# Agent attention with a squared-ReLU layer: sessions of three, three and two slots instead of two

## The chip, the cores and the metric

The kernel runs on one core of a Trainium2 chip (trn2). The metric is the device time of one execution in microseconds. Five engines work side by side, each with its own queue in order: PE (TensorE, matrix products), ACT (ScalarE), DVE (VectorE), POOL (GpSimd) and SP, which only starts DMAs. PEld stands for PE's loading of weights, which the profile lists apart. PE writes into PSUM, which has eight banks of 128 rows x 512 fp32 values; POOL works on SBUF alone.

## The reference

There are four batches of 12480 tokens of width 128, with 49 agents each, and then one layer of width 2048 over all 49920 tokens:

```python
a2k = sm(agents, k)          # softmax of agents . k / sqrt(128) over the keys
agent_v = a2k @ v
q2a = sm(q, agents)
x = (q2a @ agent_v).reshape(49920, 128)
h = np.maximum(x @ w_in, 0.0)
out = h * h @ w_out
```

Everything is fp32, and `w_in`, `w_out` come as 64-bit floats.

## The kernel before, in words

For each batch `x @ w_in` is not computed from `x`. The kernel makes a table `agent_v @ w_in` of 49 rows and 2048 columns, and the 49 attention weights of a token multiply it. To keep fp32's precision with matrix products of lower precision (`F32R`), tables, weights and squares are each split into a high part (rounded) and a low part (the rest), and products of parts are added up in PSUM. High and low rows of the attention weights and of the table are stacked: 98 rows, and of the third combination (high weights by low table) 30 rows more, which fill the 128 rows of the array. The other 19 rows of that combination have no room; they are multiplied in a small product of its own. Four copies of these 19 rows lie at rows 0, 32, 64 and 96 (tile `x`, tables `aw_ex`), so that four small products, each on 32 rows of the array, stand side by side.

The tokens are worked in groups of 960, two halves of 480 each. A **slot** is one half and two of the 16 chunks of 128 columns of `w_in`, so a half has 8 slots (`NP`) and the program 832. For each slot `k`:

- `first` multiplies: into a tile `h` of PSUM (two banks, 2 x 480 columns) go two full products of `w` and `aw_hi` and two small ones of `x` and `aw_ex`. Before, `first(k)` does so for two slots at once: four full products, then the four small ones.
- `hidden` makes `r = relu(h)` on ACT, the square on DVE as `r * h` (into SBUF tile `gg` for the even slot, back into PSUM for the odd one), its rounded high part `g_hi` as ACT's own square of `r`, and the low part `g_lo`, square less `g_hi`: two instructions of 480 columns on POOL for the even slot, one of 960 on DVE for the odd one.
- `second` multiplies the parts of the square by `wo_hi` and `wo_lo` into one bank `o`: six full products a slot, added up over the 8 slots of a half. `copied_out` then brings `o` to SBUF on DVE and out.

So a session of two slots has 16 full products of 480 columns and one set of four small ones. `second` of a slot runs `LAG` = 4 slots, two sessions, behind its `first`.

PSUM: three tiles `h` of two banks (`ps_h`), one bank for `o` (`ps_o`) and one (`ps_a`) for all other products. These others are the background: for the next batch the scores of keys, their maxima, the values and tables (`background`, paced by `goal` and `SPREAD`), and for the next group of tokens its queries (`queries`). They are cut into steps at each `yield`, and the loop at the end takes some of them in each slot. The products of `first`, the rectifications, squares, parts and `second` are chained in the order of the program on each engine (`queued`); the background's instructions, and POOL's, are placed between them by the scheduler when the program is built, and then stand fast. `first`'s small products are issued with high priority, right behind its full ones.

The prologue up to about 114 us loads and splits the weights and does the first batch's attention (`alone`).

Of the kernel before, what the change touches and what calls it, by code (L numbers as in the profile page):

```python
# [9 lines left out]
F32 = mybir.dt.float32  # L10
F32R = mybir.dt.float32r
# [6 lines left out]
P = 128  # L18
# [4 lines left out]
G = BLK // 2  # L23
RB = 2
HB = 5
LB = 4
GB = 2
LAG = 4
# [8 lines left out]
def agent_attention_relu2(ctx: ExitStack, tc: tile.TileContext, qT, kT, v, agT, w_in, w_out, outT):  # L37
# [17 lines left out]
    def queued(issue, eng, *args, **kw):  # L55

        with tc.issue_after(chain[eng]) if eng in chain else ExitStack():
            ins = issue(*args, **kw)  # L58
        chain[eng] = ins.ins
        return ins  # L60
# [315 lines left out]
    def first(k):  # L376

        g, i = divmod(k, SLOTS)
# [3 lines left out]
        hs = [ps_h.tile([P, 2, 512], F32, name="h") for _ in range(2)]  # L382
# [5 lines left out]
        with tc.high_priority():  # L388
            for t, out in enumerate(outs):
                rows = slice(t * 32, t * 32 + NL)  # L390
                queued(nc.tensor.matmul, nc.tensor, out, state[b]["lo"][rows, c // 2, :], x[rows, :], start=False, stop=True)
        return hs

    def hidden(k, h):
        r = ffn.tile([P, 2, G], F32, name="r", bufs=RB)
        queued(nc.scalar.activation, nc.scalar, r, h[:, :, :G], AF.Relu)

        gg = h[:, :, :G] if k % 2 else ffn.tile([P, 2, G], F32, name="gg", bufs=GB)
        queued(nc.vector.tensor_mul, nc.vector, gg, r, h[:, :, :G])
        hi = ffn.tile([P, 2, G], F32R, name="g_hi", bufs=HB)  # L400
        queued(nc.scalar.activation, nc.scalar, hi, r, AF.Square)
        lo = ffn.tile([P, 2, G], F32R, name="g_lo", bufs=LB)
        if k % 2:
            queued(nc.vector.tensor_sub, nc.vector, lo, gg, hi.bitcast(F32))
        else:
            for n in range(2):
                nc.gpsimd.tensor_sub(lo[:, n, :], gg[:, n, :], hi[:, n, :].bitcast(F32))  # L407
        parts[k] = hi, lo
# [108 lines left out]
    for k in range(total + LAG):  # L517
        if k < total:
# [13 lines left out]
        if k % 2 == 0:  # L532
            hs = first(k) if k < total else ()
            if hs:
                hidden(k, hs[0])
            for n in range(2):
                if k + n >= LAG:
                    second(k + n - LAG)
            copied_out()
            if hs:  # L540
                hidden(k + 1, hs[1])
# [35 lines left out]
```

## Time and profile before

| what | value |
|---|---|
| median of 3 runs | 2089.64 us (2088.23 to 2092.76) |
| the profiled execution, its own time | 2089.47 us |
| its span in the trace | 2087.6 us |
| `r`, ACT, 128x960 | 832 times, mean 962 ns |
| `g_hi`, ACT (square of `r`), 128x960 | 832 times, mean 1007 ns |
| square into PSUM (`h<-r,h`) and into SBUF (`gg<-r,h`), DVE | 416 times each, mean 1160 and 1149 ns |
| `g_lo<-h,g_hi`, DVE, 128x960 | 416 times, mean 1156 ns |
| `g_lo<-gg,g_hi`, POOL, 128x480 | 832 times, mean 1222 ns |
| full products `h<-w` and `o<-g` | 1664 and 4992 |
| small products `h<-x` | 1664 |

A group's row in the profile names the line, the engine, the operation, the tile written and those read, the shapes and the count, then the busy time and the mean of one, then the engine's idle time ahead of these instructions and what ended it. Most rows have line 58, the helper `queued`, so the tiles tell them apart. In a timeline a row has its start, its length, and the count of instructions that it merges. Recorded matmuls overlap: the next starts before the end of the last is recorded.

### The profile page before, as it was taken

Reading aid. Unit: us, or ns where it says so; the run is one execution under the profiler, and the core shown is the slowest. Engines: PE = TensorE matmul, PEld = TensorE weight load, DVE = VectorE, ACT = ScalarE, POOL = GpSimd, SP = SyncE. Lnnn points to the kernel's source line nnn. Section 1 sums busy time; section 2 is a strip of 40 time slices with the busy share of each in tenths; the row PEclk is TensorE's granted clock in tenths of the full one; section 3 lists DMA queues with packets and bytes.
Section 4 is the critical chain, followed back from the end, with each engine's and each line's share of the span. In section 5 each row is a group of like instructions: output and inputs, shape, how many; then the busy total and the mean of one; then the engine's idle time right before and its main releaser. Section 6 shows DMA issues by size and latency. Waiting matters only on the chain. (4 is left out here: it accounts for less than half of the span.)

```text
span 2087.6 us, 31676 instructions
## 1 busy us (share of the span) xinstructions
PE 2051.5 (98%) x10932; PEld 1621.5 (78%) x10932; DVE 1672.7 (80%) x1835; ACT 1775.2 (85%) x2100; POOL 1275.1 (61%) x1110
## 2 busy tenths in 40 slices
PE   8889999999999999999999999999999999999999
PEld 8857777777778877777778877777777777777777
DVE  3465888889887788888887788888888888888887
ACT  1265899989888899999898889999889999989897
POOL 1643587766554477776555458777556565656565
PEclk6588999999999999999999999999999999999999
DMA  8132222121112212221112211221111111111100
GB/s 300 46 118 87 70 75 75 52 65 63 53 56 79 65 53 80 63 60 61 63 40 71 88 35 60 68 75 41 44 51 35 46 35 47 35 47 35 38 23 20
DMA packets 55943, 131.34 MB, mean 63 GB/s; under 512 B 6712, under 2 KB 35336, under 8 KB 55784
## 3 DMA queue, kind: packets, MB, share of 16 engines
q1 hardware_dynamic: 55784, 129.33, 19.3%
q8 instruction: 87, 1.43, 0.3%
q14 instruction: 72, 0.59, 0.1%
HBM read 80.97 MB, written 25.56 MB: 51 GB/s over the span
## 5 line engine op out<-in xcount | busy, mean ns | idle before, releaser
L407 POOL TENSOR_TENSOR g_lo<-gg,g_hi 128x480 fp32r<-128x480 f32 x832 | 999.1, 1222 | 711.2 <-DVE gg L58 457.5
L58 ACT ACTIVATE r<-h 128x960 f32<-128x960 f32 x832 | 800.7, 962 | 145.5 <-PE h L58 132.7
L58 ACT ACTIVATE g_hi<-r 128x960 fp32r<-128x960 f32 x832 | 837.5, 1007 | 34.8 <-PE o L58 1.0
L58 DVE TENSOR_TENSOR h<-r,h 128x960 f32<-128x960 f32 x416 | 482.5, 1160 | 156.7 <-ACT r L58 151.6
L58 DVE TENSOR_TENSOR gg<-r,h 128x960 f32<-128x960 f32 x416 | 478.0, 1149 | 85.4 <-ACT r L58 79.9
L58 PE MATMUL o<-g_hi,wo_hi 128*128 128x480 f32 x1664 | 539.2, 405 | 0.0
L58 DVE TENSOR_TENSOR g_lo<-h,g_hi 128x960 fp32r<-128x960 f32 x416 | 481.0, 1156 | 48.3 <-ACT g_hi L58 7.7
L58 PE MATMUL h<-w,aw_hi 128*128 128x480 f32 x1664 | 485.4, 398 | 10.7 <-DVE gg L58 7.7
L58 PE MATMUL o<-g_hi,wo_lo 128*128 128x480 f32 x1664 | 495.4, 379 | 0.0
L58 PE MATMUL o<-g_lo,wo_hi 128*128 128x480 f32 x1664 | 494.7, 378 | 0.0
L58 PEld LDWEIGHTS o<-g_hi,wo_hi 128*128 128x128 f32 x1664 | 280.9, 188 | 117.4 <-issue 69.5
L58 PEld LDWEIGHTS o<-g_hi,wo_lo 128*128 128x128 f32 x1664 | 313.3, 188 | 47.2
L58 PEld LDWEIGHTS o<-g_lo,wo_hi 128*128 128x128 f32 x1664 | 313.3, 188 | 46.7
L58 PEld LDWEIGHTS h<-w,aw_hi 128*128 128x128 f32 x1664 | 289.3, 190 | 59.3 <-DVE gg L58 20.3
L58 PE MATMUL h<-x,aw_ex 19*128 19x480 f32 x1664 | 207.9, 481 | 1.3 <-DMA x<-w 1.0
L58 PEld LDWEIGHTS h<-x,aw_ex 19*128 19x128 f32 x1664 | 81.6, 182 | 142.4 <-issue 138.1
L334 PEld LDWEIGHTS psa<-ag,qt 128*120 128x120 f32 x816 | 100.6, 184 | 6.5 <-issue 0.7
L58 DVE COPY ob<-o 128x480 f32<-128x480 f32 x104 | 68.2, 656 | 35.9 <-PE o L58 35.5
L334 PE MATMUL psa<-ag,qt 128*120 128x49 f32 x816 | 95.9, 261 | 0.0
L219 POOL TENSOR_TENSOR vs<-vt,vs 128x1024 fp32r<-128x1024 f32 (+1 forms) x39 | 81.6, 2094 | 12.6 <-ACT vs L217 12.3
L183 PEld LDWEIGHTS psa<-ag,kt 128*128 128x128 f32 (+1 forms) x588 | 76.4, 195 | 3.6
L183 PE MATMUL psa<-ag,kt 128*128 128x49 f32 (+1 forms) x588 | 72.7, 271 | 0.0
(112 smaller groups left out, 1069.0 us busy)
## 6 DMA issues: line engine op xcount, KB each, us to landing
qt<-in_qT SPq DMA_DIRECT2D x52, 480.0 KB
out_T<-ob SPq DMA_DIRECT2D x104, 240.0 KB
kt<-in_kT SPq DMA_DIRECT2D x36, 512.0 KB
vt<-in_v SPq DMA_DIRECT2D x36, 512.0 KB
x<-w SPq DMA_DIRECT2D x416, 35.6 KB
ahead<-in_kT SPq DMA_DIRECT2D x12, 512.0 KB
ahead<-in_v SPq DMA_DIRECT2D x12, 512.0 KB
w<-w SPq DMA_DIRECT2D x104, 56.2 KB
```

The costliest lines, as they stand in the source:

```text
L58: ins = issue(*args, **kw)
L183: pe.matmul(sv[:, t, :], kt[:, t * rows : (t + 1) * rows], ag[:, b, :], start=True, stop=True)
L219: eng.tensor_sub(out[:, :, n : n + w], x, out[:, :, :w].bitcast(F32))
L334: pe.matmul(sv[:, t, :], qt[:, t * TP : (t + 1) * TP], ag[:, b, :], start=True, stop=True)
L407: nc.gpsimd.tensor_sub(lo[:, n, :], gg[:, n, :], hi[:, n, :].bitcast(F32))
```

## The change

Eight slots of a half are now worked in sessions of three, three and two (`RUN` = 3). `first`, `second` and the three parts of `hidden` (now `rectified`, `squared`, `split_up`) take a whole session, and `second` follows two sessions behind (`LAG` = 2). A session of three has six full products into all three tiles `h`, then its six small products. The square stays in the SBUF tile where the rectification was put (`g`, in place), for all slots; `g_hi` is a copy of it, not ACT's own square; and of a session the second slot's `g_lo` is DVE's, from two SBUF tiles, while POOL makes the first's and the third's, five of eight in all. The tile `gg` is gone, and buffers of `g_hi` and `g_lo` are 6 each.

```diff
-RB = 2
-HB = 5
-LB = 4
-GB = 2
-LAG = 4
+RUN = 3
+RB = 4
+HB = 6
+LB = 6
+LAG = 2
...
-    def first(k):
+    def first(ks):
-        g, i = divmod(k, SLOTS)
+        g, i = divmod(ks[0], SLOTS)
...
-        hs = [ps_h.tile([P, 2, 512], F32, name="h") for _ in range(2)]
+        hs = [ps_h.tile([P, 2, 512], F32, name="h") for _ in ks]
...
-            for t, out in enumerate(outs):
+            for n, out in enumerate(outs):
+                u, t = divmod(2 * c + n, NQ)
                 rows = slice(t * 32, t * 32 + NL)
-                queued(nc.tensor.matmul, nc.tensor, out, state[b]["lo"][rows, c // 2, :], x[rows, :], start=False, stop=True)
+                queued(nc.tensor.matmul, nc.tensor, out, state[b]["lo"][rows, u, :], x[rows, :], start=False, stop=True)
-    def hidden(k, h):
-        r = ffn.tile([P, 2, G], F32, name="r", bufs=RB)
-        queued(nc.scalar.activation, nc.scalar, r, h[:, :, :G], AF.Relu)
-
-        gg = h[:, :, :G] if k % 2 else ffn.tile([P, 2, G], F32, name="gg", bufs=GB)
-        queued(nc.vector.tensor_mul, nc.vector, gg, r, h[:, :, :G])
-        hi = ffn.tile([P, 2, G], F32R, name="g_hi", bufs=HB)
-        queued(nc.scalar.activation, nc.scalar, hi, r, AF.Square)
-        lo = ffn.tile([P, 2, G], F32R, name="g_lo", bufs=LB)
-        if k % 2:
-            queued(nc.vector.tensor_sub, nc.vector, lo, gg, hi.bitcast(F32))
-        else:
-            for n in range(2):
-                nc.gpsimd.tensor_sub(lo[:, n, :], gg[:, n, :], hi[:, n, :].bitcast(F32))
-        parts[k] = hi, lo
+    def rectified(hs):
+        gs = []
+        for h in hs:
+            g = ffn.tile([P, 2, G], F32, name="g", bufs=RB)
+            queued(nc.scalar.activation, nc.scalar, g, h[:, :, :G], AF.Relu)
+            gs.append(g)
+        return gs
+
+    def squared(ks, hs, gs):
+        for h, g in zip(hs, gs):
+            queued(nc.vector.tensor_mul, nc.vector, g, g, h[:, :, :G])
+
+    def split_up(ks, gs):
+        for n, (k, g) in enumerate(zip(ks, gs)):
+            hi = ffn.tile([P, 2, G], F32R, name="g_hi", bufs=HB)
+            queued(nc.scalar.copy, nc.scalar, hi, g)
+            lo = ffn.tile([P, 2, G], F32R, name="g_lo", bufs=LB)
+            if n == 1:
+                queued(nc.vector.tensor_sub, nc.vector, lo, g, hi.bitcast(F32))
+            else:
+                for m in range(2):
+                    nc.gpsimd.tensor_sub(lo[:, m, :], g[:, m, :], hi[:, m, :].bitcast(F32))
+            parts[k] = hi, lo
...
-    for k in range(total + LAG):
-        if k < total:
+    sessions = [
+        range(k + n, min(k + n + RUN, k + NP)) for k in range(0, total, NP) for n in range(0, NP, RUN)
+    ]
+    for s in range(len(sessions) + LAG):
+        ks = sessions[s] if s < len(sessions) else ()
+        for k in ks:
...
-        if k % 2 == 0:
-            hs = first(k) if k < total else ()
-            if hs:
-                hidden(k, hs[0])
-            for n in range(2):
-                if k + n >= LAG:
-                    second(k + n - LAG)
-            copied_out()
-            if hs:
-                hidden(k + 1, hs[1])
+        if ks:
+            hs = first(ks)
+            gs = rectified(hs)
+            squared(ks, hs, gs)
+        if s >= LAG:
+            for k in sessions[s - LAG]:
+                second(k)
+        copied_out()
+        if ks:
+            split_up(ks, gs)
```

PE's queue late in the last batch, before: one session of two slots, with `h` numbered by its buffer; `x2` counts the two products of a slot.

```order
L58 MATMUL h_20864<-w1_20582,aw_hi_15370 128x480 x2
L58 MATMUL h_20865<-w1_20582,aw_hi_15370 128x480 x2
L58 MATMUL h_20864<-x1_20583,aw_ex_15371 128x480 x2
L58 MATMUL h_20865<-x1_20583,aw_ex_15371 128x480 x2
L58 MATMUL o_20806<-g_hi_20801,wo_hi_108 128x480 x2
L58 MATMUL o_20806<-g_hi_20801,wo_lo_109 128x480 x2
L58 MATMUL o_20806<-g_lo_20803,wo_hi_108 128x480 x2
L58 MATMUL o_20806<-g_hi_20822,wo_hi_108 128x480 x2
L58 MATMUL o_20806<-g_hi_20822,wo_lo_109 128x480 x2
L58 MATMUL o_20806<-g_lo_20824,wo_hi_108 128x480 x2
```

The same queue of the changed kernel near its end, a session of three and the first two slots of the `o` products behind it:

```order
L58 MATMUL h_20549<-w1_20235,aw_hi_15086 128x480 x2
L58 MATMUL h_20550<-w1_20235,aw_hi_15086 128x480 x2
L58 MATMUL h_20551<-w1_20235,aw_hi_15086 128x480 x2
L58 MATMUL h_20549<-x1_20236,aw_ex_15087 128x480 x2
L58 MATMUL h_20550<-x1_20236,aw_ex_15087 128x480 x2
L58 MATMUL h_20551<-x1_20236,aw_ex_15087 128x480 x2
L58 MATMUL o_20521<-g_hi_20491,wo_hi_108 128x480 x2
L58 MATMUL o_20521<-g_hi_20491,wo_lo_109 128x480 x2
L58 MATMUL o_20521<-g_lo_20493,wo_hi_108 128x480 x2
L58 MATMUL o_20521<-g_hi_20496,wo_hi_108 128x480 x2
L58 MATMUL o_20521<-g_hi_20496,wo_lo_109 128x480 x2
L58 MATMUL o_20521<-g_lo_20498,wo_hi_108 128x480 x2
```

Six small products now stand in a row where four stood, between six full ones and the `o` products of a session two back. In all 832 slots there are 312 sets (208 of six, 104 of four) where there were 416 of four.

DVE's queue around one query of the last batch, before (`m`, `e`, `z` are the query's maximum, difference and sum):

```order
L58 TENSOR_TENSOR g_lo_19982<-h_19947,g_hi_19980 128x960
L337 TENSOR_REDUCE m_20436<-psa_20386 120x8
L339 TENSOR_TENSOR e_20438<-psa_20386,m_20436 120x392
L58 TENSOR_TENSOR gg_19998<-r_19996,h_19986 128x960
L58 TENSOR_TENSOR h_19987<-r_20017,h_19987 128x2x480
L344 TENSOR_REDUCE z_20480<-e_20438 120x8
L58 TENSOR_TENSOR g_lo_20022<-h_19987,g_hi_20020 128x960
```

DVE's queue of the changed kernel around a query of the last batch:

```order
L58 TENSOR_TENSOR g_lo_19682<-g_19652,g_hi_19680 128x960
L337 TENSOR_REDUCE m_20107<-psa_20042 120x8
L339 TENSOR_TENSOR e_20109<-psa_20042,m_20107 120x392
L58 TENSOR_TENSOR g_19710<-g_19710,h_19695 128x960
L344 TENSOR_REDUCE z_20112<-e_20109 120x8
L58 TENSOR_TENSOR g_19712<-g_19712,h_19696 128x960
L345 TENSOR_SCALAR z_20112<-z_20112 120x8
L58 TENSOR_TENSOR g_19714<-g_19714,h_19697 128x960
L346 RECIPROCAL z_20112<-z_20112 120x8
L58 TENSOR_TENSOR g_lo_19744<-g_19712,g_hi_19742 128x960
```

Three squares of a session stand together with one `g_lo` behind them, which reads two SBUF tiles (`g`, `g_hi`) where it read PSUM and SBUF (`h`, `g_hi`); the query's sums `z` stand between the squares.

## The prediction

> **What bounds the kernel now.** The page comes first: who is busy, and at what clock.
>
> ```profile
> PE 2051.5 (98%) x10932; PEld 1621.5 (78%) x10932; DVE 1672.7 (80%) x1835; ACT 1775.2 (85%) x2100; POOL 1275.1 (61%) x1110
> ...
> PEclk6588999999999999999999999999999999999999
> ```
>
> TensorE is busy 98% of the span and holds the full clock after the first tenth. Busy matmuls overlap, though, so the waits are read next, cut to 130 to 2087 us, behind the start.
>
> ```profile
> PE h L58 <- DVE gg L58: 7.4, 12, 1.6
> ```
>
> That is the longest wait of PE itself: 7.4 us in all for a free PSUM tile. So time is won only by giving TensorE less to do, and lost by a new wait of TensorE. What it does is read in the timeline of the last, undisturbed stretch, where two whole sessions of two slots follow each other (I read starts, since the recorded ends overlap).
>
> ```profile
> 2065.75 1.03 PE L58 MATMUL h<-w,aw_hi 128*128 128x480 f32 x4
> 2066.72 0.49 PE L58 MATMUL h<-x,aw_ex 19*128 19x480 f32 x4
> ...
> 2069.82 1.04 PE L58 MATMUL h<-w,aw_hi 128*128 128x480 f32 x4
> 2070.79 0.19 PEld L58 LDWEIGHTS h<-x,aw_ex 19*128 19x128 f32 x4 [0.34 <-issue]
> 2070.79 0.49 PE L58 MATMUL h<-x,aw_ex 19*128 19x480 f32 x4
> ...
> 2071.22 0.70 PE L58 MATMUL o<-g_hi,wo_hi 128*128 128x480 f32 x2
> ...
> 2071.76 0.59 PE L58 MATMUL o<-g_hi,wo_lo 128*128 128x480 f32 x2
> ...
> 2073.71 0.84 PEld L58 LDWEIGHTS h<-w,aw_hi 128*128 128x128 f32 x4
> 2073.93 1.02 PE L58 MATMUL h<-w,aw_hi 128*128 128x480 f32 x4
> ```
>
> A session takes 4.07 and 4.11 us, mean 4.09. From 2071.76 to 2073.93 ten full products start, 0.217 apart; the stretch before gives 0.214, so I use 0.2155. Sixteen full products make 3.45; the rest, **0.64 us, is what one set of four small products costs**. It can be seen in pieces: after 4 x 0.2155 the set would be due at 2070.68 and opens 0.11 late; its first `o` product comes 0.43 behind; and the first two `o` products take 0.70 instead of 0.59, another 0.11. A set of four thus costs as much as three full products, though its four stream side by side (0.49 us for all): most of it is the way in and out, where weights are loaded in the open.
>
> **The change, part by part.** *Fewer sets.* Eight slots had four sets and now have three: 104 x 0.64 = **-66.6 us**.
>
> *Second rounds.* In the sets of six, the fifth and sixth product use the same 32 rows as the first and second (or the third and fourth), so they cannot stream beside them. There are 208 such sets. The trace has no second round. From below, the nearest row is the pitch of products on the same rows, 0.2155; less is excluded because a row group streams 480 columns for each. From above it is a whole pass with load and way out in the open, 0.43, the interval from set to `o` above. I take 0.2155, because in the rows above the load for the `h` products starts at 2073.71, 0.22 before the first of them and while an `o` product holds all rows: loads go ahead of a stream on the same rows. 208 x 0.2155 = **+44.8 us**. The point at which these two parts cancel is 0.32 for a second round.
>
> The Trainium skill ("TensorE: Matmul & The Clock Gate", Part 3, "The mechanism") says both that weight loads are pulled ahead where they go to the background buffer and that they overlap running matmuls only where the row group differs. The full-array rows here agree with the first statement; no row shows it for 32-row tiles, and the second one would give the first rival below.
>
> *Tiles in PSUM.* All six banks of `h` are now filled by one session of three, so its products wait until the session before has left them: rectified on ACT, then multiplied on DVE. The paces for that:
>
> ```profile
> 1850.78 0.95 ACT L58 ACTIVATE r<-h 128x960 f32<-128x960 f32 x1
> 1851.63 0.52 ACT L217 CAST pp<-e 120x392 fp32r<-120x392 f32 x1
> ...
> 2065.11 0.95 ACT L58 ACTIVATE r<-h 128x960 f32<-128x960 f32 x1
> ...
> 2066.09 1.16 DVE L58 TENSOR_TENSOR h<-r,h 128x960 f32<-128x960 f32 x1 [0.61 <-ACT r L58]
> ...
> 2067.24 0.97 ACT L58 ACTIVATE r<-h 128x960 f32<-128x960 f32 x1
> 2067.39 1.16 DVE L58 TENSOR_TENSOR g_lo<-h,g_hi 128x960 fp32r<-128x960 f32 x1
> 2068.25 1.01 ACT L58 ACTIVATE g_hi<-r 128x960 fp32r<-128x960 f32 x1
> 2068.47 1.14 DVE L58 TENSOR_TENSOR gg<-r,h 128x960 f32<-128x960 f32 x1
> 2069.16 0.96 ACT L58 ACTIVATE r<-h 128x960 f32<-128x960 f32 x1
> ```
>
> The rectification starts 0.52 after its set (2066.72 to 2067.24); the next independent instruction on ACT follows a rectification after 0.85 and a square after 0.91; DVE starts 0.03 behind ACT's result and takes the next after 1.08. The new copy to `g_hi` isn't in the trace; from below, rectifications cost 0.85, from above a square 1.01; I take the square's 0.91 pitch, the same size from SBUF to SBUF. ACT's eight copies stand for eight squares, at no cost; they free it, as a square had to wait for its own rectification (2067.24 to 2068.25 is 1.01, not 0.85).
>
> Now one cycle by hand, from the start X of a set. Call the sessions A (three slots, then `o` of three), B (three, then `o` of two), C (two, then `o` of three). In A the products on DVE start at 1.52, 2.60, 3.68 and free their tiles at 2.67, 3.75, 4.83. PE opens the next session's tiles 0.54 + 0.2155 + 18 x 0.2155 = 4.63, 5.06, 5.50 after X: **0.67 to spare**. In B only 12 `o` products stand between, and C wants its two tiles at 3.34 and 3.77; they are free at 2.67 and 3.75: **nothing to spare**. C's rectifications stand behind B's three copies, ACT free at 5.80 instead of the 4.82 wanted, so its DVE products start 0.98 late, at 2.49 and 3.57; the next A wants its last tile at 5.28 and it is free at 4.72: 0.56. A quiet cycle is 6.03 + 4.30 + 5.81 = 16.14 against 16.36 for four sessions of before, and no engine is fuller than PE: ACT 8 x (0.85 + 0.91) = 14.1, DVE 11 x 1.08 + 0.66 = 12.5.
>
> *What disturbs it.* In 28 of the 208 sessions of three the order of the changed kernel puts a query's exponential between the rectifications and its sums between the products on DVE (15 in A, 13 in B). What these take is in the groups of 600 to 1100 us (count, then busy us and mean ns of one, then idle before):
>
> ```profile
> L407 POOL TENSOR_TENSOR g_lo<-gg,g_hi 128x480 fp32r<-128x480 f32 x208 | 249.7, 1222 | 168.2 <-DVE gg L58 116.5 <-ACT r L58 18.4 <-PE o L58 17.2
> ...
> L345 DVE TENSOR_SCALAR z<-z 120x8 f32<-120x8 f32 x13 | 8.0, 619 | 0.1
> ...
> L344 DVE TENSOR_REDUCE z<-e 120x8 f32<-120x392 f32 x13 | 7.2, 554 | 0.0
> ```
>
> 0.55 and 0.62 move the third product from 3.68 to 4.85 and its tile to 6.00, 0.5 past the 5.50. In two thirds of the places other work of PE stands ahead of that tile and takes the 0.5, by the order; the rest is 9 x 0.5 = **+4.7 us** (between 0 and 14).
>
> *Five of eight low parts on GpSimd, DVE's from two SBUF tiles.* By count GpSimd gets 10 x 1.22 = 12.2 us in a cycle instead of 9.8. But these rows show that it isn't alone there:
>
> ```profile
> 995.59 2.22 POOL L219 TENSOR_TENSOR vs<-vt,vs 128x1024 fp32r<-128x1024 f32 x1 [0.17 <-ACT vs L217]
> ...
> 996.45 1.51 DVE L289 TENSOR_TENSOR x<-av 98x129 f32<-98x129 f32 x1
> ...
> 1494.08 0.28 DVE L289 TENSOR_TENSOR x<-av 98x129 f32<-98x129 f32 x1
> ```
>
> The same DVE addition of two SBUF operands takes 0.28 alone and 1.51 when GpSimd is at work: it ends at 997.96, just behind GpSimd's end at 997.81. Before, DVE's `g_lo` read its square from PSUM and stayed at 1.16 throughout; now it must wait for GpSimd's instruction in flight, up to 1.22 for each of three in a cycle, and holds GpSimd for 1.08. Together 12.2 + 3.2 = 15.4 of 16.14 on that path: it fits, barely. What waits in DVE's queue behind such a `g_lo` are the next session's products. In A it asks at 5.02 and ends by 7.3, while the next product is due at 7.55. In C it asks at 5.76 and may end at 8.06 against 7.33, 0.73 late, which eats A's 0.67; then A's `g_lo` may end 0.5 late for B, where nothing is to spare. A third of the C sessions (33 of 104, by the order) have no other work of PE ahead of the second tile: 35 x half of 0.5 = **+8.7 us** (0 to 52).
>
> The Trainium skill ("SBUF — State Buffer", "Who interferes with whom") says that a DVE instruction with two SBUF inputs contends with a GpSimd instruction that reads SBUF and that whoever issues first keeps the path; the rows above agree, and the rule in full force would give the second rival.
>
> *Start.* Before the first `o`, sessions fill the PSUM twice; each time a third tile costs one more pitch of DVE, 2 x 1.08 = **+2.2 us** (0 to 4). The end has `o` products of two sessions behind the last set, so nothing waits there; a dropped buffer `gg` and more of `g_hi` and `g_lo` cost no time. The 7.4 us of old waits for tiles go (**-7.4**), as the new ones are counted.
>
> Sum: -66.6 + 44.8 + 4.7 + 8.7 + 2.2 - 7.4 = -13.6. The profiled execution took 2089.47, with a span of 2087.6 and 1.9 around it, 0.2 under the median of the runs. So **2076 us**.
>
> **Rivals.** (1) *The second round is paid in full.* If the loads of the fifth and sixth product wait for the first round, a second round costs 0.325 (0.11 more) to 0.43. Then sets give 104 x (2 x 0.325 - 0.64) = +1 to +23 us, and with the 8.2 of the other terms the time is 2099 to 2121. It speaks for it that the trace has no such round; against it, that loads run ahead everywhere else. It decides from 0.32. (2) *The path between DVE and GpSimd* sets the pace: if most `g_lo` of DVE stand their whole 1.22, every cycle loses the 0.5 at C's second tile, 52 instead of 8.7: 2119; half of it, 2093. For it: 15.4 of 16.14, and GpSimd's other work on top (its busy 1275.1 less 832 x 1.2, 277 us or 2.7 a cycle). Against it: that work falls into cycles that PE's own background stretches too. It decides where GpSimd lags more than 0.67 in most cycles. (3) *Nothing measurable*: the saving of 21.8 is real but small waits of background products on PE, whose operands GpSimd now makes later, eat it: about 2089.
>
> **How the numbers follow.** Chances: the forecast 0.50 (own range 2066 to 2088), rival 1 0.18, rival 2 0.20, rival 3 0.12. The low end is the sum without any new wait, 2089.5 - 21.8 = 2067.7, and a little of the unknown; the high end takes in most of rivals 1 and 2. 0.2% (4.2 us) is about what a measurement of this kernel can tell from no change, so "same" is 2085 to 2094. Faster: nearly all of the forecast's 0.50 and some of rival 3, 0.46; same: 0.18; slower: rivals 1 and 2 for the most part, 0.36.
>
> **What would show it.** In the timeline, six small products should take about 0.70 from their first start to the end of the last, with `o` 0.64 behind the set; 0.75 or more is rival 1. In the groups, DVE's `g_lo` should rise from 1.16 to between 1.5 and 2.0, and PE's wait for `DVE g` should be under 20 us; over 50 is rival 2, and waits of `psa` for POOL are rival 3. ACT's copies should be near 1.0 us. The forecast is wrong if a quiet cycle of eight slots takes more than 16.36 us.

## The result, and the profile after

| | median of the runs | lowest to highest |
|---|---|---|
| before | 2089.34 us (4 runs) | 2088.23 to 2092.76 |
| after | 2194.84 us (4 runs) | 2193.87 to 2195.86 |

The ratio is 1.0502, with an interval of 1.0484 to 1.052: the changed kernel is 5% **slower**, 105.5 us. The forecast was 2076 (its own range 2066 to 2088), and the dearest rival came to 2121.

The page of the changed kernel has the busy time of the engines first, then the granted clock in 40 slices, and in its chain of work that ended last the share of each engine:

```profile
PE 2086.0 (95%) x10932; PEld 1651.9 (75%) x10932; DVE 1640.8 (75%) x1731; ACT 1726.6 (79%) x2100; POOL 1798.9 (82%) x1318
...
PEclk6588899999999999999999999999999999999999
...
PE 63%; POOL 16%; ACT 7%; DVE 6%; issue 5%; DMA 1%; SPq 0%; ACTq 0%; DVEq 0%; POOLq 0%
```

PE went from 98% to 95% busy; POOL rose from 1275 to 1799 us and stands on 16% of the chain. Its groups of low parts and copies (busy, mean ns of one, idle time before them), from the view by line:

```profile
L416 POOL TENSOR_TENSOR g_lo<-g,g_hi 128x480 fp32r<-128x480 f32 x1040 | 1485.9, 1459 | 302.4 <-ACT g_hi L58 298.7 <-PE o L58 2.5 <-PE psa L201 0.8
L58 ACT CAST g_hi<-g 128x960 fp32r<-128x960 f32 x832 | 800.7, 1002 | 41.7 <-DVE g L58 29.5 <-PE o L58 6.6 <-PE h L58 0.3
L58 DVE TENSOR_TENSOR g_lo<-g,g_hi 128x960 fp32r<-128x960 f32 x312 | 473.0, 1516 | 158.5 <-ACT g_hi L58 154.3 <-PE h L58 2.4
```

Both engines' low parts became longer: GpSimd's from 1222 to 1459 ns, which over 1040 of them is 246 us, and DVE's from 1156 to 1516, 112 us over 312. The copy to `g_hi` costs what the square did. The waits (us in total, times, longest) show where that arrives:

```profile
PEld h L58 <- DVE g L58: 45.9, 98, 2.6
ACT g L58 <- POOL g_lo L416: 33.2, 60, 2.1
PE psa L356 <- POOL pp L219: 25.4, 24, 2.2
ACT d L271 <- POOL d L225: 21.1, 16, 3.0
PE o L58 <- DVE ob L58: 13.7, 17, 2.6
PE h L58 <- DVE g L58: 12.0, 21, 1.9
```

PE now waits for tiles, for `ob`, and for GpSimd's part of the queries, in many small pieces; ACT waits for buffers `g` that GpSimd still reads and for the background's differences `d`. Where the background is over, the waits stand alone. The timeline of that last stretch (start, length, engine, work, count, idle before):

```profile
2108.57 0.49 PE L58 MATMUL h<-x,aw_ex 19*128 19x480 f32 x4
...
2115.04 0.30 PEld L58 LDWEIGHTS h<-x,aw_ex 19*128 19x128 f32 x6 [0.33 <-issue]
2115.04 0.70 PE L58 MATMUL h<-x,aw_ex 19*128 19x480 f32 x6
...
2115.67 0.70 PE L58 MATMUL o<-g_hi,wo_hi 128*128 128x480 f32 x2
...
2121.05 0.70 PE L58 MATMUL h<-x,aw_ex 19*128 19x480 f32 x6
2121.64 2.70 ACT L58 ACTIVATE g<-h 128x960 f32<-128x960 f32 x3 [0.60 <-PE h L58]
...
2122.64 3.28 DVE L58 TENSOR_TENSOR g<-g,h 128x960 f32<-128x960 f32 x3 [1.08 <-ACT g L58]
...
2124.37 1.25 PE L58 MATMUL h<-w,aw_hi 128*128 128x480 f32 x4
2124.91 0.30 PEld L58 LDWEIGHTS h<-w,aw_hi 128*128 128x128 f32 x2 [0.35 <-DVE g L58]
...
2125.55 0.49 PE L58 MATMUL h<-x,aw_ex 19*128 19x480 f32 x4
2125.84 0.65 DVE L58 COPY ob<-o 128x480 f32<-128x480 f32 x1
...
2126.64 0.68 PE L58 MATMUL o<-g_hi,wo_hi 128*128 128x480 f32 x2 [0.60 <-DVE ob L58]
```

With the sessions of a half named A, B (three slots each) and C (two), set to set it is 6.47 from C to A (2108.57 to 2115.04), 6.01 from A to B, 4.50 from B to C: a quiet cycle of 17.0 us, not 16.14. Six small products take 0.70 and `o` follows 0.63 behind their start, as forecast. Two things are new. In session C the first product of the next half's `o` starts 1.09 behind the set instead of 0.43: there is one bank `o`, its copy `ob` stands on DVE behind B's three products, and PE waits 0.60 for it. And C's four full products take 1.25 instead of 1.03: the load of weights for its second tile waits for DVE's product (0.35), and the set opens 0.2 late.

Mean cycle of eight slots, worked out from the starts of the sets, in stretches of the 103 cycles (1 to 13 are the start, 14 to 65 carry background, 79 to 99 queries only, the last four nothing):

| cycles | 1-13 | 14-65 | 66-78 | 79-99 | 100-103 |
|---|---|---|---|---|---|
| before | 21.30 | 19.17 | 18.48 | 17.48 | 16.4 |
| after | 23.09 | 19.98 | 19.40 | 18.47 | 17.0 |

So 23 us went in the start, 42 in the 52 cycles with background, 12 and 21 in the next two stretches: everywhere, and more where other work is about.

Part of this is the granted clock. Its mean over the span is 0.953, where the kernel before has 0.969; from 408 to 1600 us it is 0.98 against 1.00. If the work of the span takes longer as the clock is lower, that is 2192.1 x 0.047 less 2087.6 x 0.031, some 38 of the 105.5 us. This is an estimate from above, since a wait costs no more at a lower clock, and no run here changes the clock alone.

### The profile page after: what moved, and what is told of

It is laid out like the page before. It is cut to its first block, busy times and chain, and to the rows that moved or that the text cites. A ratio compares the mean times of both kernels' runs of the same rounds, so it can differ in the third digit from the quotient of the medians.

```text
span 2192.1 us, 31058 instructions
## 1 busy us (share of the span) xinstructions
PE 2086.0 (95%) x10932; PEld 1651.9 (75%) x10932; DVE 1640.8 (75%) x1731; ACT 1726.6 (79%) x2100; POOL 1798.9 (82%) x1318
## 4 chain that ended last, share of the span: by engine, by line
PE 63%; POOL 16%; ACT 7%; DVE 6%; issue 5%; DMA 1%; SPq 0%; ACTq 0%; DVEq 0%; POOLq 0%
PE o L58 35%; PE h L58 20%; POOL g_lo L416 10%; ACT g L58 4%; DVE g L58 3%; PE psa L334 3%; PE psa L183 3%; ACT g_hi L58 2%; POOL vs L219 1%; POOL pp L219 1%; PE psa L356 1%; POOL d L225 1%; DMA x<-w 1%; POOL e L219 1%; POOL e L347 1%
## 5 line engine op out<-in xcount | busy, mean ns | idle before, releaser
L416 POOL TENSOR_TENSOR g_lo<-g,g_hi 128x480 fp32r<-128x480 f32 x1040 | 1485.9, 1459 | 302.4 <-ACT g_hi L58 298.7
L58 DVE TENSOR_TENSOR g<-g,h 128x960 f32<-128x960 f32 x832 | 924.8, 1149 | 255.7 <-ACT g L58 253.2
L58 ACT ACTIVATE g<-h 128x960 f32<-128x960 f32 x832 | 771.2, 975 | 233.0 <-PE h L58 191.8
L58 ACT CAST g_hi<-g 128x960 fp32r<-128x960 f32 x832 | 800.7, 1002 | 41.7 <-DVE g L58 29.5
L58 DVE TENSOR_TENSOR g_lo<-g,g_hi 128x960 fp32r<-128x960 f32 x312 | 473.0, 1516 | 158.5 <-ACT g_hi L58 154.3
L58 PE MATMUL o<-g_hi,wo_lo 128*128 128x480 f32 x1664 | 504.7, 384 | 0.0
L58 PE MATMUL o<-g_lo,wo_hi 128*128 128x480 f32 x1664 | 503.9, 383 | 0.0
L58 PEld LDWEIGHTS o<-g_hi,wo_hi 128*128 128x128 f32 x1664 | 295.0, 192 | 135.4 <-issue 56.6
L58 PEld LDWEIGHTS h<-w,aw_hi 128*128 128x128 f32 x1664 | 292.3, 192 | 88.0 <-DVE g L58 45.9
L334 PEld LDWEIGHTS psa<-ag,qt 128*120 128x120 f32 x816 | 105.5, 191 | 17.8 <-ACT w L361 10.8
L356 PEld LDWEIGHTS psa<-identr,pp 120*98 120x98 f32 x408 | 49.9, 169 | 44.8 <-POOL pp L219 33.1
L356 PE MATMUL psa<-identr,pp 120*98 120x120 f32 x408 | 53.2, 253 | 28.9 <-POOL pp L219 25.4
```

What stands on the lines that cost most here:

```text
L334: pe.matmul(sv[:, t, :], qt[:, t * TP : (t + 1) * TP], ag[:, b, :], start=True, stop=True)
L356: pe.matmul(pt[:K2, t * TP : (t + 1) * TP], pp[:, j * (NT // 2) + t, :], identr, start=True, stop=True)
L416: nc.gpsimd.tensor_sub(lo[:, m, :], g[:, m, :], hi[:, m, :].bitcast(F32))
```

## The experiments

The theories: (1) PE's wait for the copy `ob`; (2) DVE's low part has both operands in SBUF and shuts GpSimd out and is shut out, or, as 2b, it is the order in DVE's queue; (3) GpSimd is late and holds buffers `g`. Each run's ratio is to the kernel before, on the same chip.

### DVE's low part: left out, and with one operand

Of the second slot in each session, the low part is left out and `g_hi` taken in its place:

```diff
-            lo = ffn.tile([P, 2, G], F32R, name="g_lo", bufs=LB)
             if n == 1:
-                queued(nc.vector.tensor_sub, nc.vector, lo, g, hi.bitcast(F32))
+                lo = hi
             else:
+                lo = ffn.tile([P, 2, G], F32R, name="g_lo", bufs=LB)
```

> The changed kernel without DVE's low parts: for the second slot of a session the third pair of o products reads the high part again in place of g_lo, so PE has the same work, and the 312 DVE subtractions from two SBUF tiles are left out of the computation. DVE loses 473 us of work and GpSimd's subtractions should fall from 1459 back to 1222 ns. Theory 2: most of the 105 us come back, below 2120 us. Theory 1: the copy to ob stands ahead of the subtraction, so its wait stays; only the background's waits for late GpSimd go: 2150 to 2185 us. Theory 3: GpSimd is freed of the stretch (246 us in all), so 2140 to 2160.

Measured: 2125.26 us, ratio 1.0174 (1.0159 to 1.0189), 69.6 below the changed kernel and just above the 2120 that theory 2 gave. But that takes DVE's work away too. So next DVE writes a low part of the same size and duration from one operand, a maximum over single elements of `g_hi`; the subtraction is left out:

```diff
-                queued(nc.vector.tensor_sub, nc.vector, lo, g, hi.bitcast(F32))
+                queued(
+                    nc.vector.reduce_max, nc.vector, lo,
+                    hi.bitcast(F32).rearrange("p n (g o) -> p n g o", o=1), axis=AX.X,
+                )
```

> The changed kernel, but DVE's instruction for the low part of the second slot reads one SBUF tile instead of two: a maximum over single elements of g_hi, so that its place in DVE's queue, its wait for ACT's copy and its size stay, and the subtraction itself is left out of the computation. Theory 2a (DVE's second SBUF input and GpSimd's reads shut each other out): GpSimd's subtractions fall from 1459 to about 1225 ns, and the time is that of the run without DVE's low parts, 2110 to 2145 us. Theory 2b (the queue: DVE stands still for ACT's copy with the next session's products behind it): GpSimd may be faster, but the time stays above 2175 us.

Measured: 2134.91 us, ratio 1.0219 (1.0204 to 1.0234). The groups of this run:

```profile
L419 POOL TENSOR_TENSOR g_lo<-g,g_hi 128x480 fp32r<-128x480 f32 x1040 | 1244.9, 1229 | 520.4 <-ACT g_hi L58 518.8 <-PE psa L201 0.8
L58 DVE TENSOR_REDUCE g_lo<-g_hi 128x960 fp32r<-128x960 f32 x312 | 358.2, 1148 | 126.7 <-ACT g_hi L58 123.4
```

With DVE's instruction at the same place, of the same size and with the same wait for ACT's copy, but one operand, GpSimd is back at 1229 ns and 59.9 us are gone. So it is the second operand, not the place in the queue, that costs most: theory 2 holds, 2b falls. The mean granted clock rose to 0.962 with it; by the estimate above some 22 of the 59.9 us came back that way, behind fewer waits of PE.

### The kernel before, with all squares in SBUF

One part of the change alone, in the kernel before (the odd slot's square in SBUF instead of PSUM):

```diff
-GB = 2
+GB = 4
...
-        gg = h[:, :, :G] if k % 2 else ffn.tile([P, 2, G], F32, name="gg", bufs=GB)
+        gg = ffn.tile([P, 2, G], F32, name="gg", bufs=GB)
```

> The kernel before with one part of the change alone: all squares go to SBUF tiles gg (four of them), so DVE's low parts read two SBUF tiles; sessions, order and ACT's own square for g_hi as before. Theory 2a: DVE's g_lo rises from 1156 to about 1500 ns and GpSimd's from 1222 to about 1450-1500, and as four DVE products a cycle now stand behind it, the time rises, 2110 to 2180 us. Theory 2b (order of the change and its copies): the time stays at 2089 within 12 us.

Measured: 2162.39 us, ratio 1.0349 (1.0332 to 1.0367). Its groups, and its waits behind them:

```profile
L407 POOL TENSOR_TENSOR g_lo<-gg,g_hi 128x480 fp32r<-128x480 f32 x832 | 1123.3, 1372 | 604.4 <-DVE gg L58 426.2 <-DVE z L346 55.3 <-PE o L58 35.7
L58 DVE TENSOR_TENSOR g_lo<-gg,g_hi 128x960 fp32r<-128x960 f32 x416 | 637.6, 1533 | 52.9 <-ACT g_hi L58 10.7 <-PE o L58 3.8 <-DVE gg L58 1.0
```

```profile
PEld h L58 <- DVE gg L58: 80.0, 113, 3.0
...
PE h L58 <- DVE gg L58: 41.0, 56, 2.6
```

The same two durations rise (1156 to 1533, 1222 to 1372) without longer sessions or more work on GpSimd, and 73.2 us are lost by this edit alone. Here DVE's squares come late, and PE's wait for them grows from 7.7 us over the whole span to 41.0.

### The copy `ob` ahead of the third product

```diff
-            squared(ks, hs, gs)
+            squared(ks, hs[:2], gs[:2])
...
         copied_out()
         if ks:
+            squared(ks, hs[2:], gs[2:])
             split_up(ks, gs)
```

> The changed kernel with one move: on DVE the copy of the finished bank o to SBUF (ob) stands ahead of the session's third product, not behind it. Theory 1 (the single bank o: the next half's first o product waits for a copy that stands behind three products on DVE): in the last 80 us of the changed kernel a cycle of eight slots takes 17.0 us, and 0.66 of it is PE waiting between a set of four and the next o product. The move takes that away in all 104 cycles: 2195 - 69 = 2126 us, between 2110 and 2140, and the clean cycle falls to 16.3 or 16.4. Theory 2 (DVE and GpSimd in each other's way over SBUF): the copy is nothing but the place where the lateness of DVE shows; the wait moves to the tiles of h, and the time stays above 2170. Theory 3 (GpSimd too late for the buffers g and for the queries' products): also above 2170.

Measured: 2191.65 us, ratio 1.0492 (1.0475 to 1.051). Only 3 us: the last quiet cycles fell from 17.0 to 16.5, but cycles 27 to 39 rose from 20.34 to 21.05. A miss for theory 1 as the main cause. The same edit was then laid over the two runs without contention:

> The earlier copy of o (first experiment) and no low parts on DVE (second) together, which alone gave -3 and -70 us. If the wait for the bank o was real and only hidden behind late GpSimd and DVE (theory 1 + 2): the clean cycle falls from 17.0 to 16.2-16.5, the 0.5 to 0.66 us show in every cycle, and the time is 2055 to 2085 us, the 16 to 22 us below the kernel before that the count of sets gives. If the two are one and the same lateness (theory 2 alone): 2110 to 2130 us.

> The earlier copy of o and DVE's one-input instruction in place of the subtraction (which is left out of the computation). Theory 1 + 2a: within 20 us of the run with the earlier copy and no low parts at all, 2060 to 2095 us, since what hurts is the second SBUF input and not DVE's work. Theory 2b: 2130 us or more.

Measured: with the low part left out 2095.75 us (1.0031, 1.002 to 1.0043), 29.5 less than without the edit; with one operand 2111.07 us (1.0103, 1.0088 to 1.0118), 23.8 less. Both lie between the two ranges that were expected (up to 2085 and 2095, or from 2110 and 2130). So the wait for `ob` is worth 24 to 30 us once the contention is gone, and only 3 with it. The sets in the quiet stretch of the first of these:

```profile
2033.98 0.70 PE L58 MATMUL h<-x,aw_ex 19*128 19x480 f32 x6
...
2040.01 0.70 PE L58 MATMUL h<-x,aw_ex 19*128 19x480 f32 x6
2040.60 2.70 ACT L58 ACTIVATE g<-h 128x960 f32<-128x960 f32 x3 [0.64 <-PE h L58]
...
2043.34 1.24 PE L58 MATMUL h<-w,aw_hi 128*128 128x480 f32 x4
...
2044.51 0.49 PE L58 MATMUL h<-x,aw_ex 19*128 19x480 f32 x4
...
2050.35 0.70 PE L58 MATMUL h<-x,aw_ex 19*128 19x480 f32 x6
```

A to B 6.03, B to C 4.50, C to A 5.84, against 6.03, 4.30 and 5.81 in the prediction: only B to C is off, by C's second tile. The cycle is 16.36, that of before: 0.2 x 104 = 21 us are the whole saving of the sets.

### More buffers `g`, and sessions of two

```diff
-RB = 4
+RB = 5
...
-            ob = ffn.tile([P, G], F32, name="ob", bufs=2)
+            ob = ffn.tile([P, G], F32, name="ob", bufs=1)
```

> The changed kernel with five buffers g for four (and one buffer ob for two, to make room). In the changed kernel's trace rectifications wait 33 us in all for GpSimd to free a buffer g. Theory 3 (these waits make the products on DVE and so all else late): 20 us or more come back, 2175 us or less. Theories 1 and 2: within 10 us of 2195, since the longest such waits lie in the sessions of two, which have time to spare.

Measured: 2203.21 us, ratio 1.0551 (1.0536 to 1.0567), 8 slower. A fifth buffer `g` (at the price of one `ob`) gives nothing, though ACT's waits name it.

```diff
-RUN = 3
+RUN = 2
```

> The changed kernel with sessions of two (RUN = 2): squares stay in SBUF, DVE subtracts from two SBUF tiles, four of eight low parts on GpSimd, but sets of four small products and two slots a session as before the change. By hand DVE's copy ob then ends 4.35 us after a set and the next half's first o product is due at 4.63. Theory 1: no wait, so the time is that of the kernel before, 2080 to 2105 us. Theory 2: DVE's subtractions, four in a cycle instead of three, are still in GpSimd's way; above 2130 us.

Measured: 2279.48 us, ratio 1.0911 (1.0895 to 1.0927), the slowest of all. Going back to two slots, with the rest of the change kept, mends nothing. From the timeline of this run, the last stretch:

```profile
2200.59 2.06 ACT L58 CAST g_hi<-g 128x960 fp32r<-128x960 f32 x2 [0.62 <-DVE g L58]
2201.25 0.49 PE L58 MATMUL h<-x,aw_ex 19*128 19x480 f32 x4
...
2202.68 1.22 DVE L58 TENSOR_TENSOR g_lo<-g,g_hi 128x960 fp32r<-128x960 f32 x1 [1.06 <-ACT g_hi L58]
...
2203.83 2.20 DVE L58 TENSOR_TENSOR g<-g,h 128x960 f32<-128x960 f32 x2
...
2205.00 2.06 ACT L58 CAST g_hi<-g 128x960 fp32r<-128x960 f32 x2 [0.62 <-DVE g L58]
2205.66 0.49 PE L58 MATMUL h<-x,aw_ex 19*128 19x480 f32 x4
```

The copy that replaced ACT's own square waits for DVE's product (0.62), DVE's low part waits for the copy of the second slot (1.06), and the next products stand behind it: a ring of 4.41 us for a session, against 4.09 before. In sessions of three more `o` products stand between two sets, and in the quiet stretch of the changed kernel DVE's products wait for ACT's rectification (1.08), not behind a low part.

### The order of `o`: as many slots as the session has

```diff
+    seconds = iter(range(total))
...
-            for k in sessions[s - LAG]:
+            for k in itertools.islice(seconds, len(ks) or RUN):
```

> The changed kernel, but every session is followed by the o of as many slots as it has itself (three, three, two) instead of three, two, three. The o of a half then ends in session B and the next half's begins in C. By hand from the rows of the changed kernel: C's two tiles are wanted 4.63 and 5.06 after B's set and free at 2.7 and 3.8, so the late second tile is gone; the copy ob ends about a microsecond ahead of the next o of a new half. A quiet cycle should come out at 16.1 to 16.3 us instead of 17.0. If these two waits are what the quiet cycle lost, that much is seen in the last, undisturbed cycles. The contention of DVE's and GpSimd's low parts is left in: if it is the main loss (theory 2), the time falls only by a part of the waits' worth, to 2160 to 2185, with GpSimd's g_lo still at 1.4 us and more and DVE's at 1.5. If the order of o was the main loss, the time comes near 2100.

Measured: 2174.35 us, ratio 1.0409 (1.0394 to 1.0425), within the span that theory 2 gave; the last cycles take 16.64 in the mean. GpSimd's low parts stayed at 1442 ns. Without DVE's low parts:

> As the run before, and DVE's low parts are left out (g_hi is taken in their place, so three of eight slots have no low part of their own). With the contention, the wait for ob and the late tile all gone, the sum of the prediction is to be seen for the first time without them: a quiet cycle of 16.1 to 16.2 us and a time of 2060 to 2082, below the kernel before. If the two small-product rounds or another part of the change cost more than was put down for them, the time stays at 2090 or above, as it did with the copy ob moved and DVE's low parts left out (2095.8).

Measured: 2090.91 us over ten runs (2087.80 to 2096.94), ratio 1.001 (1.0 to 1.0021). The quiet cycle is 16.17: the sum by hand (16.14) is right once `ob` and the late tile are gone. But the time missed its 2060 to 2082 and came to the 2090 or above of the other branch. In the trace, which is of the slowest of the ten runs (2096.94), the cycles 1 to 13 take 22.35 instead of 21.30, 13.6 us, and there the trace of the changed kernel shows something not looked for. Its PE rows, and then its busy times by stretch of 10 us, with the granted clock third from the end:

```profile
216.40 1.99 PE L183 MATMUL psa<-ag,kt 128*128 128x49 f32 x16 [0.80 <-ACT w L361]
218.62 2.63 PE L58 MATMUL h<-w,aw_hi 128*128 128x480 f32 x6 [0.24 <-DMA w<-w]
221.19 0.76 PE L58 MATMUL h<-x,aw_ex 19*128 19x480 f32 x1
222.63 0.77 PE L58 MATMUL h<-x,aw_ex 19*128 19x480 f32 x1 [0.68 <-DMA x<-w]
...
226.47 0.77 PE L58 MATMUL h<-x,aw_ex 19*128 19x480 f32 x3 [1.45 <-DMA x<-w]
```

```profile
200.00:210.00 10.00, 10.00 (x66) 8.62 (x65) 8.17 (x9) 8.43 (x12) 8.48 (x8) 1.00 0.17 52
210.00:220.00 10.00, 8.96 (x50) 7.36 (x49) 6.58 (x7) 5.75 (x8) 7.76 (x6) 0.94 0.33 88
220.00:230.00 10.00, 7.86 (x21) 4.81 (x20) 2.80 (x3) 4.07 (x6) 0.00 (x0) 0.50 0.25 76
```

The queries' weights `w` and their copies `x` reach a new group's first set late, and the set breaks up. The granted clock is 0.50 over these 10 us, but it fell before the two longest waits: ahead of the set PE had waited 0.80 us for ACT's `w` and 0.24 for the DMA of `w`, the clock is 0.70 from 218 to 220, and the set's six full products already take 2.63 us, where they take 1.47 in the quiet stretch. At 270 it falls again. The kernel before has 1.0 in all stretches between 180 and 400 us. In this run without DVE's low parts the same two places have 0.85 and 0.57. No run took these waits away, so their price is read from the cycles and not shown by an experiment.

### DVE's low parts from PSUM, the computation whole

Here, with the even order of `o`, DVE takes two of eight low parts, both in session B, whose product is written over `h` and read from there (`g_hi` is then ACT's square again); GpSimd takes six:

```diff
+    def middle(ks, hs):
+        g0, g1 = rectified(hs[:2])
+        queued(nc.vector.tensor_mul, nc.vector, g0, g0, hs[0][:, :, :G])
+        queued(nc.vector.tensor_mul, nc.vector, hs[1][:, :, :G], g1, hs[1][:, :, :G])
+        hi1 = square_of(g1)
+        (g2,) = rectified(hs[2:])
+        lo1 = rest_of(hs[1], hi1)
...
+        queued(nc.vector.tensor_mul, nc.vector, hs[2][:, :, :G], g2, hs[2][:, :, :G])
```

> The whole computation, with sessions and o as in the even order. DVE takes low parts only in session B, of its second and third slot, and reads their squares from PSUM, where the product is written over h (two of eight instead of three; GpSimd takes six). If the second SBUF operand of DVE's low part is what shuts the two engines out, GpSimd's g_lo goes back to 1.22 to 1.26 us and DVE's to 1.16, and the time comes to 2070 to 2100, near or below the kernel before. If GpSimd's load by itself were the trouble (six of eight low parts, 14.7 us of a cycle), it would be slower than the even order with DVE's low parts from SBUF, and PE would wait for g_lo.

Measured: 2177.97 us, ratio 1.0425 (1.0407 to 1.0442). The low parts were undisturbed (1154 and 1228 ns) and yet nothing was won over the even order (2174.35), as the expectation had it for GpSimd's load. But PE's wait for `ob` was back too, 0.60 a quiet cycle, since the copy stood behind the third product. With the first and third slot instead, and `ob` ahead of the third product:

> The whole computation. As the run with two of DVE's low parts read from PSUM, but they are taken of the first and third slot of session B, and the copy ob stands ahead of the third product on DVE. In the run before, a quiet cycle took 17.0: 0.60 of it PE's wait for ob, 0.2 the late second tile of C, though no low part was slowed down (1.15 and 1.23 us). By hand the two tiles are free at 3.75 and 4.83 after B's set (wanted 4.63 and 5.06) and ob ends before C's o. If those two waits are what was left, a quiet cycle is 16.2 to 16.4 and the time falls by 0.6 to 0.8 for each of 104 cycles, to 2090 to 2115: the contention removed and the work kept. If GpSimd's load (six of eight low parts) is a bound by itself in the stretches with background, these stay at 19.5 to 20.3 a cycle and the time at 2140 or above.

Measured: 2174.70 us, ratio 1.0395 (1.0378 to 1.0413). By the numbers of the expectation that speaks for GpSimd's load. But the trace has six stops of PE of 6.4 to 6.8 us from start to start, between 817 and 1480 us (and three of 3.2 to 3.4), and the timeline of one shows their cause:

```profile
894.45 7.09 POOL L414 TENSOR_TENSOR g_lo<-g,g_hi 128x480 fp32r<-128x480 f32 x6
...
895.14 7.32 DVE L346 TENSOR_SCALAR z<-z 120x8 f32<-120x8 f32 x1
...
901.46 0.97 POOL L226 TENSOR_TENSOR d<-s,mb 128x392 f32<-128x392 f32 x1
902.38 1.15 DVE L59 TENSOR_TENSOR h<-g,h 128x960 f32<-128x960 f32 x1
...
904.87 1.17 PE L59 MATMUL h<-w,aw_hi 128*128 128x480 f32 x2 [6.03 <-DVE g_lo L59]
```

An addition to eight numbers a row, SBUF to SBUF, takes 7.32 us, where its shortest takes 0.16 (the median of its 52 is 0.16 in the kernel before, 0.78 in this run): it ends at 902.46, when GpSimd's unbroken row of seven instructions ends (902.43), and the products of the next tiles stand behind it. So this run can't tell. Two edits take that stop away, in this kernel and in the even order of `o`:

```diff
-HB = 6
+HB = 7
...
-        dve.tensor_scalar_add(z, z, 1e-9)
...
-            ob = ffn.tile([P, G], F32, name="ob", bufs=2)
+            ob = ffn.tile([P, G], F32, name="ob", bufs=1)
```

> The whole computation: as the run before (two of DVE's low parts from PSUM, in session B, six on GpSimd), with a seventh buffer g_hi (one ob less) and without the addition of 1e-9 to the query's sums z. Those sums hold a one, so the addition changes nothing in single precision; the instruction is left out because it stood up to 7.39 us behind an unbroken row of GpSimd's low parts, with PE stopped for 6 us at eight places. If these long stops and the copy to g_hi that waited for o (59 us in all) are what kept the run at 2174.7, this comes to 2095 to 2125, with undisturbed low parts of 1.15 and 1.23 us and no stop of PE over 3 us. If six low parts on GpSimd are too many in the stretches with background by themselves, it stays at 2140 or above with the cycles there at 19.3 to 20.5.

> The whole computation: the even order of o with the same two edits (seventh g_hi, one ob, no addition to z), but DVE's three low parts read from SBUF, five on GpSimd. Against the run it goes with, only the low parts differ. If the shutting out of DVE's and GpSimd's low parts costs by itself, this one is slower by 30 to 70 us (2140 to 2175) with GpSimd's at 1.44 and DVE's at 1.5 us; if not, the two are within 10 us of each other.

Measured: 2116.85 us, ratio 1.0135 (1.012 to 1.015), with low parts from PSUM, and 2150.42 us, ratio 1.0291 (1.0274 to 1.0308), from SBUF. That is 57.9 and 23.9 less than without the two edits, which were not tried apart. The groups, of the first and then of the second:

```profile
L413 POOL TENSOR_TENSOR g_lo<-g,g_hi 128x480 fp32r<-128x480 f32 x1248 | 1491.6, 1233 | 265.7 <-ACT g_hi L59 259.6 <-ACT s L187 1.6 <-PE psa L278 0.7
L59 DVE TENSOR_TENSOR g_lo<-h,g_hi 128x960 fp32r<-128x960 f32 x208 | 240.6, 1157 | 21.6 <-DVE h L59 0.5 <-PE o L59 0.2 <-ACT g_hi L59 0.2
```

```profile
L416 POOL TENSOR_TENSOR g_lo<-g,g_hi 128x480 fp32r<-128x480 f32 x1040 | 1481.1, 1456 | 241.8 <-ACT g_hi L59 238.1 <-PE o L59 2.7
L59 DVE TENSOR_TENSOR g_lo<-g,g_hi 128x960 fp32r<-128x960 f32 x312 | 486.8, 1560 | 131.5 <-ACT g_hi L59 101.3 <-PE psa L335 11.1 <-PE h L59 7.3
```

GpSimd is busy with low parts equally long in both, 1492 and 1481 us: six undisturbed ones cost it as much as five that are shut out. At that load the kernel with undisturbed parts is 33.6 us faster, though its quiet cycle is the longer one (16.97 against 16.54). So GpSimd's load by itself does not hold the time at 2150; what is shut out on DVE, with the next session's products behind it, costs too. How the 59.9 us of the run with one operand divide between GpSimd's lateness and DVE's stays open: these two kernels also differ in the order on ACT and DVE, and DVE takes two low parts a cycle in the first and three in the second.

Last, DVE's low parts of the second and third slot, with these edits and `ob` ahead of the third product:

```diff
+    def middle(ks, hs):
+        g0, g1 = rectified(hs[:2])
+        squared(ks[:1], hs[:1], [g0])
+        in_place(hs[1], g1)
+        hi1 = square_of(g1)
+        (g2,) = rectified(hs[2:])
+        parts[ks[1]] = hi1, rest_of(hs[1], hi1)
+        hi2 = square_of(g2)
```

> The whole computation: as the run of 2116.9 us (low parts from PSUM, seventh g_hi, no addition to z), with DVE's low parts taken of the second and third slot of session B, so that C's first tile is freed by the first product, and the copy ob ahead of the third product. In the run before, a quiet cycle took 16.9, of it 0.32 PE's wait for C's second tile and 0.2 to 0.4 for A's tiles behind the late products of C. By hand from its rows the second tile is now free 5.14 after B's set and wanted at 4.94, and C's products start 0.2 late instead of 0.6. A quiet cycle of 16.4 to 16.6 is expected, 0.3 to 0.5 less in 104 cycles: 2065 to 2090, at or below the kernel before. If the tiles of PSUM are not what is left (the start's late x and lower clock, or GpSimd's load), it stays at 2105 or above.

Measured: 2138.65 us, ratio 1.0237 (1.0223 to 1.0251): a miss, 22 slower than the run that it should have mended. The quiet cycle stayed at 16.9 (C's second tile 0.25, A's third 0.24 late). Why the stretches with background also got longer was not followed; in the traces ACT's wait for buffers `g` that GpSimd still reads rises from 5.0 to 33.8 us, and PE has one stop of 6.2 us at 312 us. No version here beats the kernel before.

## Why the prediction was wrong, step by step

**What held.** A set of six costs what was forecast: `o` starts 0.63 behind the first small product where it was 0.43 behind a set of four, so a second round takes 0.2, a little under the 0.2155 taken, and the first rival is out. The Trainium skill ("TensorE: Matmul & The Clock Gate", Part 3, "The mechanism") says that loads overlap only where the row group differs; these second rounds, on the same 32 rows, don't bear that out: at 2115.04 all six loads are done 0.30 after the first began, while a small product takes 0.49. The copies cost 1.00 us. A to B took 6.01 to 6.03 (6.03 forecast), and C to A, with `ob` moved, 5.84 (5.81). DVE's `g_lo` came to 1.516, inside the 1.5 to 2.0.

**The step that failed** is "Five of eight low parts on GpSimd, DVE's from two SBUF tiles", put at +8.7 us (0 to 52). The mechanism was named, and its mark, DVE's duration, was right; its price was not. Taking the second operand away gave 59.9 us, leaving the instruction out 69.6, and the one edit in the kernel before cost 73.2. The sum priced only the second tile of C in 33 sessions, by DVE's lateness, and kept GpSimd at 1.22 for its own part ("12.2 + 3.2 = 15.4 of 16.14"). (It also multiplied 35 sessions where it had counted 33.) Measured, GpSimd's low parts alone are 1485.9 / 104 = 14.3 us a cycle, and 313 us of other work add 3.0: 17.3 in the mean. From 408 to 1600 us GpSimd is busy 87% of the time, where it was 64%. It is not full, but it runs behind at places, and what stands behind it in its queue (`pp`, `e`, `d`) comes late to ACT and PE, beside the buffers `g`. That these waits make up the price is argued from the trace; shown is the price of the operand. The load alone is not the price either: with as many microseconds of low parts on GpSimd, none of them shut out, the kernel with the two further edits came to 2116.85. The prediction had this load in its second rival, at 2119 at most. Both the second rival's mark (PE's wait for `DVE g`, under 20 or over 50) and the third's (`psa` for POOL) showed in part: 12.0 on PE, with 45.9 on PE's loads, and 25.4. The loss shows at several waits, and only one of them was priced.

The Trainium skill ("SBUF — State Buffer", "Who interferes with whom") says that with two SBUF inputs DVE contends with GpSimd's reads and with one it does not: the run with one operand (1229 and 1148 ns) agrees. It also counts the kind of small addition made on `z` among those that may contend, and says that whoever issues first keeps the path for the whole instruction; here DVE was kept out for seven of GpSimd's instructions, not one.

**A wait that wasn't seen.** The prediction walked through PE's tiles `h` and DVE's count, but not through the bank `o`. With one bank, the next half's `o` can't start before `ob` has been copied, and the change put that copy behind three products: 0.66 a quiet cycle, 24 to 30 us in the runs without contention. With one operand and `ob` moved, 59.9 and 23.8 of the 105.5 us are accounted for by edits, in runs that leave DVE's subtraction out. Of the 21.7 left, 10.4 are in the first 13 cycles of that run and 7.8 in the 52 with background.

**A term with nothing to spare.** B to C was given "nothing to spare". After a set of six the rectification starts 0.59 to 0.62 behind the set's first product, not the 0.52 read after a set of four, which makes C's second tile 0.05 to 0.08 late by the figures of the sum. The rest of the 0.2 lies at the load of weights: the sum asked when the product wants its tile, but the load ahead of the product waits for the tile (the row at 2124.91), and then stands in the open. The 0.2 in each of 104 cycles is about the 21.8 us of the sets. With the even order of `o` and without DVE's low parts the cycle was 16.17.

**The start** was put at +2.2 us; the first 13 cycles lost 23, of which 13.6 remain without DVE's low parts. Late `x` and the lower clock stand at that place; their share is argued from the trace alone. By the granted clock, 0.90 over these 300 us against 0.96 over the 277 before, the estimate is some 19 of the 23. **The old waits for tiles** (-7.4) were not won, since new ones took their place. **Buffers**: a fifth `g` gave nothing. The terms for queries (+4.7) were not measured apart.

## What to carry to other kernels

When an operand moves from PSUM to SBUF, price both engines that share the path: multiply what one instruction of each becomes longer by its whole count, add the other work in its queue, and compare that with the cycle. Then list every wait that stands behind these two engines, not only the nearest one. When sessions are made longer, walk through every single buffer (the bank `o` here), and read the latency behind the new, longer group, not the old one, and ask for a tile at the load ahead of the product. A spare time of zero is a term of its own: its sign decides about the whole gain.

## What the hardware showed that was not expected

- DVE and GpSimd both lose when their low parts meet: 1156 to 1516 ns and 1222 to 1459 ns in the mean. A DVE instruction can be kept out for an unbroken row of GpSimd's: 7.32 us for an addition that takes 0.16 at its shortest.
- The granted clock fell to 0.50 from 220 to 230 us behind waits of PE of 0.80 and 0.24 us, where the kernel before had 1.0; the waits of 0.68 and 1.45 us came when it was down. What sets it off is not shown. The mean over the span was 0.969 before and 0.953 after.
